# Attention products on TensorE tiles of 64 rows by 32 columns in place of 64 by 64

## The chip, the cores and the metric

The kernel runs on one core of a Trainium2 chip. The metric is the device time of one execution in microseconds. The kernel before takes 577.24 us, the median of three runs (577.07 to 577.51).

## What is computed

Attention with a sliding window and a linear position bias, followed by a gated MLP with spatial mixing. All inputs and outputs are float32. The shapes: 8 batches, 8 heads, 576 positions, 64 dimensions a head; the MLP has a model width of 512 and an inner width of 1024.

```python
def _attn_ref(q, k, v):
    B, H, S, D = q.shape
    window = 128
    scores = (1.0 / np.sqrt(D)) * np.matmul(q, k.transpose(0, 1, 3, 2))
    rel = np.arange(S)[:, None] - np.arange(S)[None, :]
    slopes = 2.0 ** (-8.0 * (np.arange(H) + 1) / H)
    bias = slopes[:, None, None] * (-np.abs(rel))[None, :, :]
    mask = (rel >= 0) & (rel < window)
    scores = np.where(mask, scores + bias[None], -1000000000.0)
    attn = softmax(scores)            # max, exp, sum, with 1e-9 added to the sum
    return np.matmul(attn, v)

def _moe_ref(x, w_in, g_ln, w_sg, b_sg, w_out):
    h = gelu_tanh(x @ w_in)
    u, v = h[..., :d_ff // 2], h[..., d_ff // 2:]
    v_n = (v - mean(v)) / np.sqrt(var(v) + 1e-06) * g_ln
    v_s = np.einsum('ts,bsd->btd', w_sg, v_n) + b_sg[None, :, None]
    return x + (u * v_s) @ w_out
```

A query at position s sees the keys s - 127 to s. So a block of 64 queries that begins at q0 needs the keys q0 - 127 to q0 + 63, at most 192 with the rounding to blocks, and a block of 32 needs at most 160.

## The kernel before, in words

The attention works on pairs of heads: 32 pairs n, four for each batch. The positions are cut into blocks of R = 64 (S = 576 is nine of them). For each pair there are single-letter steps: `q` and `L` load q, k and v; `a` and `c`, or `*` for both in one burst, make the scores; `A`, `B`, `C`, `G` (`minima`) add the bias and find each row's extreme; `e`, `E`, `f`, `F`, `j` take exponentials; `R` inverts the sums; `r`, `s`, `S` scale; `t`, `T`, `z` transpose on TensorE; `X`, `Y` mask; `V` (`values`) multiplies with v; `x`, `2`, `p` gather the result; `h`, `l`, `k` split it into a high and a low part for the MLP. The MLP of each batch follows in steps of its own (lines 609 to 611, 907, 942, 943, 1061), three products for each product of float32 accuracy.

The order of all steps is written out by hand in one long string, `ORDER`. On each engine instructions run in that order; the only freedom is when an engine waits for another. From pair 5 on, the scores of a pair are one step `*` (n >= 5), before that two steps `a` and `c`. For 16 of the later pairs the step `V` of pair n is written straight behind `*` of pair n + 2, and there the product of the first block of 64 positions goes into spare columns of that pair's last score bank.

Scores (`score_list`, lines 264 to 291). For t2 = 0 and t2 = 2 two PSUM banks of 512 columns are taken. A product has 64 queries of one head as its stationary operand (64 rows by 64 columns of the array) and up to 192 keys as its moving one. Head j lies on the rows j * 64 to j * 64 + 63, and its output goes to partitions 0 to 63 or 64 to 127, by `half ^ j`, so four tiles of the array are used. For each t2 there are eight products (two blocks i, two halves, two heads), and for t2 = 0 two more of 64 columns for the first 64 queries, which for `*` come before those of t2 = 2. In all 18 products a pair; each is float32 and shows as two matmul records and two weight loads. `burst` keeps the written order within a step.

Minima (`minima`, lines 297 to 307, on VectorE). In a bank the window of block i begins at column i * 192; the parts of the window that the mask cuts (the oldest and the own block) share 64 columns: `copy_predicated` puts the visible elements of the own block over the oldest one, so that 128 columns are left, on which two reductions run (a third for the first 64 queries).

Values (`values`, lines 368 to 392). The stationary operand is v (64 positions by 64 dimensions of one head), the moving one the masked, transposed weights of up to three blocks of queries, so up to 192 columns. Odd blocks k use the array's rows 0 to 63 and bank `x1[0]`, even ones rows 64 to 127 and bank `x1[1]`; the head gives the column half: again four tiles. Nine blocks by two heads are 18 products, and `first` adds two of 64 columns.

```python
for half in range(2):
    for j in range(2):
        q0 = (2 * t2 + 1 + i + 2 * half) * R
...
            insts.append(score(half, j, i * W, q0, q0 - P, q0 + R))
...
burst([part(k, c) for k in (0, 1, 2 * T, *range(2, 2 * T)) for c in cols] + [first(c) for c in cols])
```

## Time and profile before

| | us |
|---|---|
| median of three runs | 577.24 |
| lowest, highest | 577.07, 577.51 |
| the profiled execution's own time | 576.7 |
| its span in the profile | 575.0 |
| mean granted clock of TensorE | 0.997 |

The profile records every instruction of one execution. Engines are PE (TensorE's matmuls), PEld (its weight loads, which overlap the matmuls), DVE (VectorE), ACT (ScalarE), POOL (GpSimd) and SP (SyncE). A matmul's record is longer than the time for which it holds its tile: the records of consecutive matmuls overlap, so starts are to be compared, not ends. A line such as L278 is the line of the kernel in which the instruction was made. "Released by" is worked out from semaphores.

### The profile page before, as it was taken

To read this page: it belongs to the slowest core of one execution; us is meant where nothing else is said; L and a number is where in the kernel's file an instruction comes from. 1 tells how busy PE (TensorE), PEld (TensorE's weight loads), DVE (VectorE), ACT (ScalarE), POOL (GpSimd) and SP (SyncE) were. 2 spreads that over 40 slices of the span, in tenths; PEclk is the share of its full clock that TensorE was granted. 3 is DMA by queue.
4 is the path that set the end of the run, shared out by engine and by line. 5 is a ranking of instruction groups with operands and counts; after the bars stand their busy time and mean duration, and the time that the engine had idled before them with its cause. 6 is when DMAs were issued, how large, how long until landed. Compare 5 with 4: busy or idle time off the path is not lost.

```text
span 575.0 us, 14661 instructions
## 1 busy us (share of the span) xinstructions
PE 560.0 (97%) x5495; PEld 510.0 (89%) x5495; DVE 474.0 (82%) x1324; ACT 378.3 (66%) x1063; POOL 307.2 (53%) x365
## 2 busy tenths in 40 slices
PE   5899999999999999999999999999999999999997
PEld 4677899998899789998999998998999999998997
DVE  8989998799989778999787987878897988575646
ACT  7998997466844867567777576646695666733422
POOL 3676646520436544575338753496348653576325
PEclk9899999999999999999999999999999999999999
DMA  8675213216404413554260554136431606012502
GB/s 301 194 231 200 79 57 104 68 68 224 166 38 149 133 38 99 163 186 120 65 218 1 166 180 175 42 103 183 124 112 65 216 1 198 2 39 93 172 1 82
DMA packets 43561, 69.78 MB, mean 121 GB/s; under 512 B 3554, under 2 KB 31202, under 8 KB 43492
## 3 DMA queue, kind: packets, MB, share of 16 engines
q1 hardware_dynamic: 43492, 68.86, 36.7%
q8 instruction: 43, 0.70, 0.5%
q14 instruction: 26, 0.21, 0.1%
HBM read 56.27 MB, written 12.58 MB: 120 GB/s over the span
## 4 chain that ended last, share of the span: by engine, by line
PE 89%; DVE 4%; ACT 4%; DMA 2%; issue 1%; POOL 0%; SPq 0%; DVEq 0%; ACTq 0%
PE ps_m L609 13%; PE ps_m L1061 13%; PE ps_m L611 12%; PE ps_m L610 12%; PE ps_m L907 12%; PE ps_a L347 5%; PE ps_a L278 4%; PE ps_s L278 4%; PE ps_m L384 3%; PE ps_s L384 3%; PE ps_m L942 2%; PE ps_m L943 2%; ACT e L311 1%; PE ps_m L798 1%; PE ps_m L800 1%; DMA wst<-w_in 1%
## 5 line engine op out<-in xcount | busy, mean ns | idle before, releaser
L334 POOL TENSOR_TENSOR e<-e,rr 128x256 f32<-128x256 f32 (+2 forms) x116 | 80.6, 717 | 96.4 <-DVE rr L323 84.0
L311 ACT ACTIVATE e<-e,stats 128x128 f32<-128x128 f32 (+1 forms) x288 | 110.7, 387 | 17.2 <-DVE stats L295 16.6
L224 POOL TENSOR_TENSOR region<-u,region 128x288 fp32r<-128x288 f32 (+1 forms) x78 | 77.7, 1016 | 44.5 <-ACT region L1008 16.2
L356 DVE TENSOR_TENSOR px<-ps_a,m_both 128x1024 f32<-128x1024 f32 x64 | 77.4, 1216 | 5.4 <-PE ps_a L347 4.7
L609 PE MATMUL ps_m<-ws,region 128*128 128x288 f32 x256 | 78.3, 306 | 0.0
L611 PE MATMUL ps_m<-ws,region 128*128 128x288 f32 x256 | 75.9, 296 | 0.0
L610 PE MATMUL ps_m<-ws,region 128*128 128x288 f32 x256 | 75.6, 295 | 0.0
L732 POOL TENSOR_TENSOR rs<-rs,mhalf 128x1 f32<-128x1 f32 (+1 forms) x40 | 30.2, 756 | 57.5 <-DVE rs L729 57.3
L218 POOL TENSOR_TENSOR xs<-xf,xs 128x288 fp32r<-128x288 f32 (+1 forms) x48 | 49.9, 1060 | 13.8 <-ACT xs L403 13.8
L311 ACT ACTIVATION_READ_ACCUMULATOR e<-e,stats 128x1 f32 x288 | 54.5, 189 | 0.0
L1008 ACT ACTIVATE region<-u 128x576 fp32r<-128x576 f32 x35 | 23.7, 684 | 43.1 <-PE ps_m L610 17.5
L609 PEld LDWEIGHTS ps_m<-ws,region 128*128 128x128 f32 x256 | 48.3, 189 | 1.6 <-issue 0.8
L610 PEld LDWEIGHTS ps_m<-ws,region 128*128 128x128 f32 x256 | 48.3, 189 | 0.1
L611 PEld LDWEIGHTS ps_m<-ws,region 128*128 128x128 f32 x256 | 48.1, 188 | 0.2 <-DVE region L744 0.2
L609 PE MATMUL ps_m<-wi,xs 128*128 128x512 f32 x112 | 46.7, 417 | 0.1
L1068 DVE TENSOR_TENSOR xf<-ps_m,xf 128x576 f32<-128x576 f32 x48 | 35.8, 750 | 10.4 <-PE ps_m L1061 9.7
L611 PE MATMUL ps_m<-wi,xs 128*128 128x512 f32 x112 | 44.3, 396 | 0.0
L610 PE MATMUL ps_m<-wi,xs 128*128 128x512 f32 x112 | 44.2, 395 | 0.0
L347 PE MATMUL ps_a<-ident,e 128*128 128x128 f32 x256 | 38.6, 277 | 1.0 <-DVE px L356 1.0
L948 DVE TENSOR_TENSOR u<-ps_m,u 128x576 f32<-128x576 f32 x32 | 24.0, 753 | 18.2 <-PE ps_m L943 11.6
L278 PE MATMUL ps_s<-qk 64*64 64x192 f32 (+2 forms) x576 | 32.2, 338 | 5.5 <-DMA qk<-qkT 4.6
L295 DVE CUSTOM_DVE_ANT_0 e<-ps_s,bias 128x128 f32<-128x128 f32 (+1 forms) x140 | 34.9, 287 | 2.5
(217 smaller groups left out, 1591.8 us busy)
## 6 DMA issues: line engine op xcount, KB each, us to landing
qk<-qkT SPq DMA_DIRECT2D x32, 576.0 KB, 4.9
sum<-store SPq DMA_DIRECT2D x36, 512.0 KB, 4.7
outT<-xf SPq DMA_DIRECT2D x31, 288.0 KB, 3.0
vt<-v_in SPq DMA_DIRECT2D x32, 256.0 KB, 4.2
wst<-w_in SPq DMA_DIRECT2D x8, 512.0 KB, 5.2
store<-sum SPq DMA_DIRECT2D x6, 512.0 KB, 2.8
vt<-v_in SPq DMA_DIRECT2D x64, 32.0 KB, 3.8
wst<-w_out SPq DMA_DIRECT2D x4, 512.0 KB, 3.6
```

Source lines behind the costliest of these rows:

```text
L218: (engine or nc.gpsimd).tensor_tensor(out[:, cs], a[:, cs], b[:, cs], op)
L224: nc.gpsimd.tensor_tensor(out[:, fs], a[:, fs], b[:, fs], ALU.subtract)
L278: return lambda: nc.tensor.matmul(banks[half][to, c:c + k1 - k0], qk[js, 0, q0:q0 + R], qk[js, 1, k0:k1], start=True, stop=True)
L311: nc.scalar.activation(x, x, AF.Exp, bias=self.nm[0:n, i:i + 1], scale=-1.0, accum_out=self.sm[0:n, i:i + 1])
L334: nc.gpsimd.tensor_tensor(x[:, z:z + step, :], y[:, z:z + step, :], self.rr[0:n, i + z:i + z + min(k, step)].rearrange("p (m o) -> p m o", ...
L347: burst([lambda t=t: nc.tensor.transpose(cv[:, t // 2, t % 2], self.pr[j][:, t, :].rearrange("p (h c) -> p h c", h=2), ident[:, j * R:j * ...
L356: nc.vector.tensor_tensor(xv, cv, mv, ALU.mult)
L609: nc.tensor.matmul(dst, ah, bh, start=(first and i == 0), stop=False)
L610: nc.tensor.matmul(dst, ah, bl, start=False, stop=False)
L611: nc.tensor.matmul(dst, al, bh, start=False, stop=(last and i == n - 1))
L907: nc.tensor.matmul(dst, left(n, g, c)[:, ms], right(n, h, c), start=first and c == 0 and k == 0, stop=c == 1 and k == 2, skip_group_check= ...
L1061: nc.tensor.matmul(dst, p, q, start=first and f == 0 and k == 0, stop=f == 1 and k == 2, skip_group_check=True)
```

## The change

Scores and values are cut to tiles of 64 rows by 32 columns. A score product takes 32 queries and up to 160 keys; there are twice as many. A window is now laid out in the bank with a step of 160 columns (`BAND`), the rows of the second 32 queries 32 columns further on, and the first 64 queries' scores begin at column 352 (`LEAD`). For t2 = 0 the blocks i are taken in the order 1, 0, and the products of the first 64 queries come at the very end of the burst. `minima` addresses the same amounts of data through a new helper `window`. In `values` v is cut to 32 dimensions a product; the blocks k come in the order 1 to 7, 0, 8, the last together with the product of the first block. The string `ORDER` is not touched.

```diff
     XW = 2 * S + R
+    BAND = 5 * R // 2
+    LEAD = 2 * BAND + R // 2
+
+    def window(bank, c0, c1):
+        x = bank[:, c0:c0 + R].rearrange("p (t c) -> p t c", t=1)
+        return bass.AP(tensor=x.tensor, offset=x.offset, ap=[x.ap[0], [c1 - c0, 2], x.ap[2]])
...
         def scores(self, *t2s):
-            burst([x for t2 in t2s for x in self.score_list(t2, ps_a if len(t2s) > 1 and t2 == 0 else ps_s)])
+            insts = [x for t2 in t2s for x in self.score_list(t2, ps_a if len(t2s) > 1 and t2 == 0 else ps_s)]
+            burst(insts + (self.last_scores if 0 in t2s else []))
...
-            W = 3 * R
...
-            def score(half, j, c, q0, k0, k1):
-                js, to = heads[j], heads[half ^ j]
-                return lambda: nc.tensor.matmul(banks[half][to, c:c + k1 - k0], qk[js, 0, q0:q0 + R], qk[js, 1, k0:k1], start=True, stop=True)
+            half_block = R // 2
+
+            def score(half, j, c, q, k0, k1):
+                js, to = heads[j], heads[half ^ j].start + q % R
+                return lambda: nc.tensor.matmul(banks[half][to:to + half_block, c:c + k1 - k0], qk[js, 0, q:q + half_block], qk[js, 1, k0:k1], start=True, stop=True)
...
-            for i in range(2):
+            for i in (1, 0) if t2 == 0 else (0, 1):
                 for half in range(2):
                     for j in range(2):
-                        q0 = (2 * t2 + 1 + i + 2 * half) * R
-                        if q0 < P:
-                            insts.append(score(half, j, i * W + R, q0, 0, P))
-                        else:
-                            insts.append(score(half, j, i * W, q0, q0 - P, q0 + R))
+                        for z in (0, half_block):
+                            q0 = (2 * t2 + 1 + i + 2 * half) * R
+                            lo = max(q0 + z - P, 0)
+                            insts.append(score(half, j, i * BAND + lo - q0 + P, q0 + z, lo, q0 + z + half_block))
             if t2 == 0:
-                insts += [score(0, j, 2 * W, 0, 0, R) for j in range(2)]
+                self.last_scores = [score(0, j, LEAD, z, 0, R) for j in range(2) for z in (0, half_block)]
...
-            sv = bank.rearrange("p (b c) -> p b c", c=R)
             alone = t2 + j == 0
-            nc.vector.copy_predicated(sv[:, 0:6:5, :], sel_first if alone else sel, sv[:, 2:4, :])
+            nc.vector.copy_predicated(window(bank, 0, BAND + P), sel_first if alone else sel, window(bank, P, BAND))
...
-                self.shift(pr[j][:, t2 + i, :].rearrange("p (b c) -> p b c", b=2), sv[:, 4 * i:4 * i + 2, :], bs, nm[:, j * T + t2 + i:j * T + t2 + i + 1])
+                c = i * (BAND + R)
+                self.shift(pr[j][:, t2 + i, :].rearrange("p (b c) -> p b c", b=2), bank[:, c:c + P].rearrange("p (b c) -> p b c", c=R), bs, nm[:, j * T + t2 + i:j * T + t2 + i + 1])
...
-                self.shift(self.e0[:, R:P], sv[:, 6, :], bias[:, 0, :], nm[:, 2 * T:2 * T + 1])
+                self.shift(self.e0[:, R:P], bank[:, LEAD:LEAD + R], bias[:, 0, :], nm[:, 2 * T:2 * T + 1])
...
-                rows, slot, cs = slice(i * R, (i + 1) * R), (k + 1) // 2, slice(c, c + WIDE)
+                rows, slot, cs = slice(i * R, (i + 1) * R), (k + 1) // 2, slice(c, c + wide)
...
-                return lambda: nc.tensor.matmul(x1[i][cs, lo * R:hi * R], vt[rows, slot, cs], px[...], start=k < 2, stop=k in (2 * T - 2, 2 * T - 1), skip_group_check=True)
+                return lambda: nc.tensor.matmul(x1[i][cs, lo * R:hi * R], vt[rows, slot, cs], px[...], start=k in order[:2], stop=k in order[-2:], skip_group_check=True)
...
-            WIDE = D
-            cols = [c for j in (1, 0) for c in range(j * D, (j + 1) * D, WIDE)]
-            burst([part(k, c) for k in (0, 1, 2 * T, *range(2, 2 * T)) for c in cols] + [first(c) for c in cols])
+            wide = D // 2
+            order = [*range(1, 2 * T), 0, 2 * T]
+            cols = [c for j in (1, 0) for c in range(j * D, (j + 1) * D, wide)]
+            burst([part(k, c) for k in order[:-1] for c in cols] + [x for c in cols for x in (first(c), part(2 * T, c))])
```

## Rows read from the trace of the kernel before

**Rows 1.** The page, engines: busy us (share of the span) x instructions.
```profile
PE 560.0 (97%) x5495; PEld 510.0 (89%) x5495; DVE 474.0 (82%) x1324; ACT 378.3 (66%) x1063; POOL 307.2 (53%) x365
```

**Rows 2.** The page, the chain that ended last, share of the span by engine.
```profile
PE 89%; DVE 4%; ACT 4%; DMA 2%; issue 1%; POOL 0%; SPq 0%; DVEq 0%; ACTq 0%
```

**Rows 3.** Busy time by stretch: length, PE, PEld, DVE, ACT, POOL, clock, DMA, GB/s.
```profile
60.00:100.00 40.00, 40.00 (x450) 36.15 (x449) 36.50 (x113) 34.59 (x103) 24.66 (x24) 1.00 0.27 82
100.00:150.00 50.00, 50.00 (x527) 44.39 (x526) 44.67 (x138) 30.79 (x93) 16.55 (x19) 1.00 0.39 131
...
200.00:250.00 50.00, 50.00 (x518) 46.40 (x517) 41.17 (x125) 32.45 (x98) 25.45 (x26) 1.00 0.32 98
```

**Rows 4.** All waits of TensorE after 60 us: us in total, times, longest.
```profile
PE ps_m L907 <- PE ps_m L907: 0.9, 1, 0.9
PE ps_a L278 <- DMA qk<-qkT: 0.2, 1, 0.2
```

**Rows 5.** Timeline of TensorE, 229.2 to 231.3 us: start, us, line, operation, count.
```profile
229.01 0.30 PE L942 MATMUL ps_m<-wsA,vA 128*128 128x288 f32 x1
229.14 0.29 PE L943 MATMUL ps_m<-wsB,vB 66*128 66x288 f32 x1
229.37 0.88 PE L278 MATMUL ps_a<-qk 64*64 64x128 f32 x20
230.08 0.82 PE L278 MATMUL ps_s<-qk 64*64 64x192 f32 x16
230.83 0.40 PE L609 MATMUL ps_m<-ws,region 128*128 128x288 f32 x1
231.07 0.29 PE L610 MATMUL ps_m<-ws,region 128*128 128x288 f32 x1
```

**Rows 6.** Groups by line and shape, TensorE: busy us, mean ns of one | idle.
```profile
L384 PE MATMUL ps_m<-px,vt 64*64 64x192 f32 x408 | 25.3, 323 | 0.0
...
L384 PE MATMUL ps_m<-px,vt 64*64 64x128 f32 x136 | 13.1, 271 | 0.0
...
L384 PE MATMUL ps_m<-px,vt 64*64 64x64 f32 x68 | 4.8, 217 | 0.0
```

**Rows 7.** The same groups, weight loads of 128 and of 64 columns.
```profile
L609 PEld LDWEIGHTS ps_m<-ws,region 128*128 128x128 f32 x256 | 48.3, 189 | 1.6 <-issue 0.8 <-DVE u L948 0.3
...
L384 PEld LDWEIGHTS ps_m<-px,vt 64*64 64x64 f32 x612 | 20.7, 133 | 1.6 <-issue 0.2
```

**Rows 8.** Score records in the first 0.03 us of a burst: length, PE (records), PEld (records).
```profile
217.64:217.67 0.03, 0.03 (x4) 0.03 (x4) 1.00 0.00 0
```

**Rows 9.** Score products (L278) by stretch, the same columns.
```profile
60.00:250.00 190.00, 18.61 (x432) 13.55 (x432) 1.00 0.33 107
250.00:482.00 232.00, 22.96 (x540) 16.90 (x540) 1.00 0.39 125
```

**Rows 10.** Value products (L384) by stretch, the same columns.
```profile
60.00:250.00 190.00, 16.80 (x396) 12.30 (x396) 1.00 0.33 107
250.00:482.00 232.00, 22.23 (x540) 18.48 (x540) 1.00 0.39 125
482.00:515.00 33.00, 3.05 (x72) 2.21 (x72) 1.00 0.14 45
```

**Rows 11.** Timeline of TensorE, 478.2 to 481.9 us, scores of pair 31 and values behind.
```profile
479.20 0.82 PE L278 MATMUL ps_s<-qk 64*64 64x192 f32 x16
479.85 1.48 PE L384 MATMUL ps_m<-px,vt 64*64 64x192 f32 x36
```

**Rows 12.** Timeline of VectorE, 228.9 to 231.3 us: the first copy after a score burst.
```profile
230.33 0.30 DVE L302 COPY_PREDICATED ps_a<-sel,ps_a 128x128 f32<-128x128 uint8 x1 [1.16 <-PE ps_a L278]
```

**Rows 13.** Line 302 (the copy): its engine's idle before it, us, times.
```profile
  PE ps_a L278: 4.0, 4
  PE ps_s L278: 1.7, 2
```

**Rows 14.** Timeline of TensorE, 72.2 to 73.0 us: four transposes, untiled.
```profile
72.30 0.66 PE L347 MATMUL ps_a<-ident,e 128*128 128x128 f32 x4
```

## The prediction

> **What bounds the kernel now.** I read the busy times first, then the chain that ended last, then the busy time by stretch, then the waits. TensorE is busy for 560.0 of 575.0 us, VectorE for 474.0 [rows 1]; the chain is TensorE for 89% [rows 2]. A busy share alone would not prove a bound, since pipelined matmuls overlap in the records. But from 60 us on there is no hole: TensorE fills the stretches of 40 or 50 us to the hundredth [rows 3], and the list of what TensorE waited for after 60 us holds 1.1 us in all [rows 4]. So a nanosecond taken off TensorE's own stream after 60 us is a nanosecond of the span, until something else comes late. Nearest to that is VectorE: 36.5 of 40 us and 44.7 of 50 us up to 150 us, 41.2 of 50 later [rows 3]. Its steps stand in the same written order and move up with the matmuls they wait for.

> The attention products are the part that changes. A score burst of one pair is 36 matmul records (18 products in two passes each), 20 of them for query blocks 0 to 3 and then 16; the matmul before it starts at 229.14 and plain spacing is back at 231.07 [rows 5]: 1.93 us for what would be two plain steps, L943 to L609 to L610, of 0.13 us (L942 to L943 is 0.13). The burst thus takes some 1.67 us out of the chain. How much of that is streaming? The passes of the values product give the rate: 323, 271 and 217 ns for 192, 128 and 64 columns [rows 6], so (323 - 217) / 128 = 0.83 ns a column and pass, 1.66 ns for both passes. On each of the four tiles of 64x64 a pair streams 768 columns of scores (half 0: 128 + 192 + 64 + 192 + 192; half 1: four times 192; the granted clock is 1.00 in these stretches [rows 3], its upper level): 1.27 us. The remaining 0.40 us is the change of tiling on both sides, the first weights, and the spread of the starts. The four tiles do run at the same time: 36 passes of mostly 0.16 us of streaming would take over 5 us one after another.

> **The change part by part.**

> *Scores.* A block of 32 queries can see 128 + 32 = 160 keys; a block of 64 is given 192. There are now eight tiles (two heads by four blocks of 32 output rows), each with these columns: half 0, first 32 rows: 160 + 96 + 160 + 160 + 64 = 640; half 0, second 32 rows: 160 + 128 + 160 + 160 + 64 = 672; half 1: four times 160 = 640. The longest tile falls from 768 to 672. If eight tiles run side by side as four do, that is 96 x 1.66 = 159 ns less a pair. Weights: 128 columns load in 189 ns, 64 in 133 [rows 7], 56 ns for 64 columns, so a load of 32 is 28 ns shorter; only a burst's first is in the open: -28 ns. Four more tiles must be started: four matmuls and four loads are under way within 0.03 us of a burst's start [rows 8], at most 7.5 ns a pair of load and matmul, so at most +30 ns. Net -0.157, call it -0.16 us a pair. After 60 us there are 432 + 540 records [rows 9], over 36 = 27 pairs: 27 x 0.16 = 4.3 us. The five pairs before 60 us lie where the chain is not TensorE's alone; I count them at nothing (bound: 5 x 0.16 = 0.8 us gained).

> *Values.* Here only the tile's width changes, not the columns. A high tile (rows 64 to 127) streams 128 + 3 x 192 + 64 = 768 columns before and after, a low one 3 x 192 + 128, and the first block's 64 more. Per burst: -28 ns for the first weights where it doesn't follow scores directly, up to +30 ns for four more tiles. Zero, with 0.04 us either way as bounds; 396 + 540 + 72 records after 60 us [rows 10], over 36 = 28 pairs: -1.1 to +1.1 us. The new order of k (1 to 7, then 0, then 8 with the first block) gives both halves of the array equal lengths at each step, as the old one did in sum; I give it nothing by itself. What it keeps is the passage from scores to values: the last 16 score records start at 479.20, values at 479.85, with no hole between [rows 11], since both run in one tiling. With 64x32 for both that stays; it would be lost if only one had changed.

> *VectorE.* The predicated copy reads and writes the same 128x128 elements at other offsets; the three reductions keep their shapes: nothing. But the last two score products (now four), which write the same bank as the first block's, move from before the second 16 records to the very end of the burst. The first copy now starts at 230.33 [rows 12], 0.96 us after the burst's start at 229.37, and about 0.3 us after the last of the 20 started (group end 229.37 + 0.88, less a pass of 0.22). Afterwards the burst's last start is some 1.14 us in (672 columns, 1.11, plus load and spread, less the last 64 columns) and the copy some 1.44: 0.48 us later. Behind it on VectorE's queue stand the other copies and reductions of the pair and whatever block work is written next; ScalarE's exponentials wait for them. VectorE stood idle at that point 4 times for ps_a and 2 for ps_s, 5.7 us in all [rows 13]. Bounds: 0 (VectorE has 9% to 18% of slack) and 6 x 0.48 = 2.9 us (every such wait reaches TensorE). TensorE almost never waits for VectorE [rows 4], so I take 0.3 us.

> *Records.* 18 more score products and 20 more value products a pair, two passes each: 38 x 2 x 32 = 2432 more matmuls on the 5495 [rows 1], as many weight loads. They cost what is above if they are fed in time.

> *Sum.* Of 4.3 us I let 85% through (bounds 60% and 100%: TensorE is nearly the whole chain after 60 us [rows 4], but the written order has links that are just in time), 3.65, less 0.3: 3.3 us. The profiled execution took 576.7 us with its span of 575.0, so 573.4; the median of the runs shown, 577.24, is 0.5 above it, so 573.9.

> [...] In the first 0.03 us of a burst four matmuls are under way [rows 8], so starts on different tiles come 10 ns apart or nearer. [...]

> **The rivals.**
> - *Feeding (slower).* With eight tiles a pair of load and matmul must be issued every 134 / 8 = 16.7 ns (a pass of 160 columns is 133 ns), where now it is one every 1.21 / 36 = 34 ns (36 starts from 229.37 to 230.08 + 0.82 - 0.32 [rows 5]). If the steady pace is p, scores last 72 p and values 80 p, against 1.37 and 1.38 us now (first load to end of streaming: 1.21 + 0.16, and about the same for values). Over 27 and 28 pairs the change breaks even where 4184 p = 75.5 us: p = 18 ns. At 20 ns it loses 8.2 us: 585; at today's 34 ns 67 us: 644. The same holds if weight loads stop being hidden: ten passes a tile, each exposed by over 9 ns, and the gain is gone. For it: the densest places, scores straight into values [rows 11], would hold 304 records in 2.6 us, twice what the trace has anywhere. Against it: the starts of [rows 8].
> - *Shared stream (the change doesn't do what it says).* Four column tiles read the same 64 rows with four different moving operands; the trace shows two. If four share what serves two, scores take 2 x 1.11 and values 2 x 1.27: 27 x 0.95 + 28 x 1.27 = 61 us slower, 638. Against it: two share nothing measurable. An untiled transpose of 128 columns takes (0.66 - 0.28) / 3 = 0.13 us from start to start, first weights included [rows 14], no quicker a column than the tiled passes.
> - *Given back.* The gain is there on TensorE, but the later copy and VectorE up to 150 us (89 to 91% busy) take it: 4.3 - 2.9 - 1.1 leaves 0.3: 577.
> - *More.* The values gain their 0.04 as well and everything passes: 4.3 + 1.1 + 0.5 of the first pairs' 0.8: 571.3.

> **How the numbers follow.** Forecast (571.9 to 575.9) 0.60; more 0.06; given back, 575.9 to 578.5, 0.14; feeding 0.15, of which a fifth under 580; shared stream 0.05. Range 571.2 to 580.0: 0.60 + 0.05 + 0.14 + 0.03, 0.82. A measurement tells 0.2%, 1.15 us, from no change. Faster by more: 0.60 + 0.06 + 0.01 = 0.67. Within: 0.12. Slower by more: 0.15 + 0.05 + 0.01 = 0.21.

> **What would show it.** Right: a score burst with 72 records in place of 36 that takes 1.77 us between plain matmuls in place of 1.93, passes of 160 columns of about 296 ns, weight loads of about 105 ns, value bursts with 80 records as long as before, and the first copy some 1.4 us after the burst's start with TensorE still without holes. Feeding shows as starts 18 ns apart or more all through a burst; a shared stream as rounds of eight passes twice 134 ns. Given back shows as new holes on TensorE with VectorE as releaser. Wrong in size: pass-through, or the 0.40 us beside the streaming, which I leave as it is.

## The result, and the profile after

The changed kernel takes 584.71 us (median of 4 runs, 583.26 to 586.07) against 577.36 us (577.07 to 577.51) for the kernel before: the ratio is 1.0128 [1.0104, 1.0152], slower. The profiled execution is one of 585.54 us with a span of 583.7. The runs of one kernel now lie 2.8 us apart, where those of before lie 0.4 us apart. In the code after, the scores' matmul is L286 (L278 before), the values' are L391 and L395 (L384, L388), the copy is L308 (L302), the MLP's are L617 to L619 (L609 to L611), the transposes L354 and L367 (L347, L360).

Rows of the profile's page of after: engines, the queue that brings TensorE's instructions, and the chain by engine.

```profile
PE 558.8 (96%) x7927; PEld 510.2 (87%) x7927; DVE 473.6 (81%) x1324; ACT 379.0 (65%) x1063; POOL 308.8 (53%) x365
...
q8 instruction: 62, 1.02, 0.7%
...
PE 83%; DVE 7%; DMA 3%; POOL 2%; ACT 2%; issue 2%; SPq 1%; DVEq 0%; POOLq 0%; ACTq 0%
```

The 2432 additional matmuls are there, as many as were counted, and TensorE is busy 1.2 us less than in [rows 1]. But its share of the chain falls from 89% in [rows 2] to 83%, and VectorE's, DMA's and "issue" grow. So the loss is in idle time, not in work. The waits of TensorE after 60 us (total, times, longest), of which [rows 4] had two:

```profile
PE ps_s L395 <- issue: 1.8, 1, 1.8
PE ps_a L286 <- DMA qk<-qkT: 1.2, 2, 1.0
PE ps_m L915 <- issue: 1.1, 1, 1.1
PE ps_m L618 <- issue: 0.5, 1, 0.5
PE ps_a L354 <- POOL e L341: 0.5, 1, 0.5
PE ps_m L1069 <- issue: 0.5, 1, 0.5
PE ps_a L367 <- DVE px L363: 0.5, 1, 0.5
PE ps_a L354 <- DVE stats L302: 0.4, 1, 0.4
PE ps_m L617 <- DVE u L956: 0.4, 1, 0.4
```

The L915 row is the L907 row of [rows 4] and not new. The others are of two kinds. "Issue" is idle time in which TensorE waits for nothing that the profile shows: there is no releaser. Such idle time within a stream is called a hole here. The rest names VectorE, GpSimd or a transfer: work that now comes late. The longest hole after 60 us, in the timeline of TensorE, in the last products of a value burst:

```profile
487.89 0.27 PE L391 MATMUL ps_m<-px,vt 64*32 64x64 f32 x2
489.95 0.24 PE L395 MATMUL ps_s<-p,vt 64*32 64x64 f32 x1 [1.79 <-issue]
```

What can stop an engine in the middle of a burst whose operands have long been there? I counted all of TensorE's records (weight loads, matmuls and the 199 of its sequencer) in order of their starts. In order of time, the holes that begin at 33.0 (2.45 us from start to start), 450.9 (0.75), 468.3 (0.98) and 488.0 (the one above, 2.01) lie at records 960, 13504, 14016 and 14528, all of them 192 above a multiple of 256 to within two records; a fifth, of 0.33 us, is at 258.2, record 7616. The queue row gives the rest: 62 packets with 1.02 MB are 16.4 KB each, and the 16053 records less the first 192 are 256 a packet (before: 43 packets for 11205 records, 256 as well). So instructions arrive in blocks of 256 records, called pages from here on, and TensorE stood still at page ends: ahead of 489.95 an instruction packet starts at 487.44, takes 1.08 us, and work goes on 1.43 us after its end; for 450.9 and 468.3 it is 1.39 and 1.37 us. Scores straight into values hold 304 records in 2.6 us; the quickest page took 9.05 us before and 2.25 us after.

How long a hole is follows from how early the packet of the next page starts. At the four it starts 0.1, 1.9, 1.8 and 0.5 us ahead of the page's end; lead and hole together are 2.6, 2.6, 2.8 and 2.5 us. Over after and the runs e3, e4 and e9 below, 25 page ends had a packet with a lead under 2.45 us, and at each the sum is 2.2 to 2.8 us; the kernel before and e1, e2, e5 and e8, none of which has such a hole, have no lead under 2.55 us. So a page that is used up quickly is only one way to a hole: the page that ends at 33.0 lasted 5.97 us, but its successor's packet started 5.8 us into it. Long leads left no such hole: the shortest in before is 8.7 us, and at after's other page ends, with leads of 3.1 us and more, TensorE's records start at most 0.24 us apart.

A score burst by itself did what was forecast. One of them, timeline of TensorE, to be laid beside [rows 5]:

```profile
232.48 0.29 PE L951 MATMUL ps_m<-wsB,vB 66*128 66x288 f32 x1
232.70 0.75 PE L286 MATMUL ps_a<-qk 64*32 64x160 f32 x29
...
233.76 0.30 PE L286 MATMUL ps_a<-qk 64*32 64x64 f32 x7
234.00 0.40 PE L617 MATMUL ps_m<-ws,region 128*128 128x288 f32 x1
234.23 0.29 PE L618 MATMUL ps_m<-ws,region 128*128 128x288 f32 x1
```

From the matmul before it to plain spacing it is 1.75 us (232.48 to 234.23) where it was 1.93; 72 passes start within 1.145 us, 16 ns apart. VectorE's first copy of this pair, in VectorE's timeline, and, from the view of line 308, the idle time ahead of all ps_a copies after 60 us (us, times), which in the same stretch of before was 3.4 in 3 (the 4.0 in 4 of [rows 13] are of the whole run):

```profile
234.16 0.30 DVE L308 COPY_PREDICATED ps_a<-sel,ps_a 128x128 f32<-128x128 uint8 x1 [1.65 <-PE ps_a L286]
```

```profile
  PE ps_a L286: 9.8, 12
```

The copy starts 1.46 us after the burst's first product (232.70), where it was 0.96: later by 0.50 us. So it is, or by up to 0.65, in 13 of the bursts after 60 us; in most of the others VectorE came to the copy over 1 us into the burst before too.

### The profile page after: what moved, and what is told of

Same layout as the page of the kernel before. It is cut to its first block, busy times and chain, and to the rows that moved or that the text cites. A ratio compares the mean times of both kernels' runs of the same rounds, so it can differ in the third digit from the quotient of the medians.

```text
span 583.7 us, 19512 instructions
## 1 busy us (share of the span) xinstructions
PE 558.8 (96%) x7927; PEld 510.2 (87%) x7927; DVE 473.6 (81%) x1324; ACT 379.0 (65%) x1063; POOL 308.8 (53%) x365
## 3 DMA queue, kind: packets, MB, share of 16 engines
q1 hardware_dynamic: 43492, 68.86, 36.5%
q8 instruction: 62, 1.02, 0.7%
## 4 chain that ended last, share of the span: by engine, by line
PE 83%; DVE 7%; DMA 3%; POOL 2%; ACT 2%; issue 2%; SPq 1%; DVEq 0%; POOLq 0%; ACTq 0%
PE ps_m L1069 12%; PE ps_m L915 12%; PE ps_m L617 11%; PE ps_m L619 11%; PE ps_m L618 11%; PE ps_a L354 5%; PE ps_m L391 4%; PE ps_s L391 3%; PE ps_a L286 3%; PE ps_s L286 2%; DMA wst<-w_in 2%; DVE e L302 2%; PE ps_m L950 1%; PE ps_m L951 1%; PE ps_m L806 1%
## 5 line engine op out<-in xcount | busy, mean ns | idle before, releaser
L230 POOL TENSOR_TENSOR region<-u,region 128x288 fp32r<-128x288 f32 (+1 forms) x78 | 78.0, 1019 | 44.9 <-ACT region L1016 16.4
L617 PE MATMUL ps_m<-ws,region 128*128 128x288 f32 x256 | 78.3, 306 | 0.4 <-DVE u L956 0.4
L619 PE MATMUL ps_m<-ws,region 128*128 128x288 f32 x256 | 76.0, 297 | 0.0
L617 PEld LDWEIGHTS ps_m<-ws,region 128*128 128x128 f32 x256 | 48.3, 189 | 1.4 <-DVE u L956 0.5
L617 PE MATMUL ps_m<-wi,xs 128*128 128x512 f32 x112 | 46.6, 417 | 2.3 <-ACT xf L373 2.2
L619 PEld LDWEIGHTS ps_m<-ws,region 128*128 128x128 f32 x256 | 48.1, 188 | 0.7 <-DVE region L752 0.6
L619 PE MATMUL ps_m<-wi,xs 128*128 128x512 f32 x112 | 44.3, 395 | 0.1
L354 PE MATMUL ps_a<-ident,e 128*128 128x128 f32 x256 | 38.9, 276 | 2.4 <-DVE px L363 1.1
L286 PE MATMUL ps_s<-qk 64*32 64x160 f32 (+3 forms) x1152 | 32.0, 305 | 5.2 <-DMA qk<-qkT 4.6
L302 DVE CUSTOM_DVE_ANT_0 e<-ps_s,bias 128x128 f32<-128x128 f32 (+1 forms) x140 | 34.9, 287 | 2.5
```

Source lines behind the costliest of these rows:

```text
L230: nc.gpsimd.tensor_tensor(out[:, fs], a[:, fs], b[:, fs], ALU.subtract)
L286: return lambda: nc.tensor.matmul(banks[half][to:to + half_block, c:c + k1 - k0], qk[js, 0, q:q + half_block], qk[js, 1, k0:k1], start=Tru ...
L354: burst([lambda t=t: nc.tensor.transpose(cv[:, t // 2, t % 2], self.pr[j][:, t, :].rearrange("p (h c) -> p h c", h=2), ident[:, j * R:j * ...
L617: nc.tensor.matmul(dst, ah, bh, start=(first and i == 0), stop=False)
L619: nc.tensor.matmul(dst, al, bh, start=False, stop=(last and i == n - 1))
```

## The experiments

In each kernel the same MLP matmuls and transposes run in the same order, so every one can be paired with its counterpart in the trace of before, and the offset between the two followed. The table splits the final offset (us): what stood at 60 us, what the bursts' own steps changed after 60 us (only steps under 0.2 us: scores alone, 13 places; scores with values behind them, 15 places; values alone, 13 places), and all else, which is waits and holes. Waits are more than the lists show, since a delay of under 0.2 us stands in no list.

| kernel | at 60 us | scores alone | scores into values | values alone | waits and holes | at the end |
|---|---|---|---|---|---|---|
| after | 1.88 | -1.69 | -0.55 | 0.72 | 8.56 | 8.92 |
| e1_scores_narrow | -0.41 | -1.67 | -0.18 | 0.04 | 3.92 | 1.70 |
| e2_values_narrow | 0.13 | 0.03 | 2.64 | 0.65 | 0.00 | 3.45 |
| e4_last_scores_early | 2.22 | -0.62 | -0.60 | 0.66 | 6.79 | 8.45 |
| e5_narrow_scores_last_early | 0.07 | -0.59 | 1.06 | -0.01 | 0.53 | 1.06 |
| e8_narrow_scores_lead_in_other_bank | -0.23 | -1.81 | -0.28 | -0.01 | 0.76 | -1.57 |
| e9_after_lead_in_other_bank | 0.80 | -1.83 | -0.61 | 0.65 | 4.98 | 3.99 |

Two theories could explain the loss: F, that TensorE runs out of instructions at page ends where records stand too densely; and D, that work behind VectorE's later copies arrives too late.

**One half of the change at a time.** Only the scores on tiles of 64x32, values as before (last lines of the diff from after; `...` stands for lines left out):

```
...
-            wide = D // 2
-            order = [*range(1, 2 * T), 0, 2 * T]
...
-            burst([part(k, c) for k in order[:-1] for c in cols] + [x for c in cols for x in (first(c), part(2 * T, c))])
+            WIDE = D
...
+            burst([part(k, c) for k in (0, 1, 2 * T, *range(2, 2 * T)) for c in cols] + [first(c) for c in cols])
```

> The changed kernel with its values put back on 64x64 tiles in the old order; only the scores are on 64x32. Theory F (TensorE's instructions are fetched in pages of 256 records, and a page used up in under some 4.4 us leaves TensorE without instructions): scores followed by values are 144 + 80 = 224 records in place of 304, so no hole of over 0.3 us at a page's end is left; 27 score bursts at -0.17 us give 4.6 us, the change of tiling between scores and values costs some 0.2 us at 16 places, 3.2 us: 576 us. Theory D (the loss comes from the first scores' last products standing at the end of the burst, so that VectorE's first copy starts 0.5 us later): it is still late here, 580 us or more.

Measured: 579.06 us (578.28 to 579.33), ratio 1.0035 [1.0023, 1.0047]. And only the values on 64x32, scores as before (last lines of the diff from before):

```
...
-            WIDE = D
...
-            burst([part(k, c) for k in (0, 1, 2 * T, *range(2, 2 * T)) for c in cols] + [first(c) for c in cols])
+            wide = D // 2
+            order = [*range(1, 2 * T), 0, 2 * T]
...
+            burst([part(k, c) for k in order[:-1] for c in cols] + [x for c in cols for x in (first(c), part(2 * T, c))])
```

> The kernel before with only its values on 64x32 tiles in the new order. Theory F: 72 + 160 = 232 records behind each other, no holes at page ends; 28 value bursts at +0.05 us, 1.4 us, and 16 changes of tiling, 3.2 us: 582 us. Theory D: the copies start as before, so at most the 1.4 us: 577 to 579 us.

Measured: 580.27 us (579.78 to 580.44), ratio 1.0058 [1.0043, 1.0073]. Neither number was met: e1 lies between its two forecasts and so does e2. But neither trace has a hole over 0.3 us at a page end after 60 us. With 224 and 232 records where after has 304, their quickest pages took 4.98 and 4.73 us, so by the page theory it takes both halves together, and that is what happened. As a limit F's 4.4 us is not shown: in after pages of 2.25, 2.94 and 3.00 us left gaps of 0.22, 0.05 and 0.23 us. What e2 costs is all in the table's tile columns: 2.64 us at 15 passages from 64x64 to 64x32, 0.18 us each, where the first value products no longer start beside the last scores (0.25 us behind the last of them where it was 0.15), and 0.65 us at 13 lone value bursts, 0.05 us each. Its waits of TensorE are those of [rows 4] to 0.1 us. In e1 the bursts give 1.8 us and something else takes 3.9. Its waits of TensorE after 60 us, and its idle time ahead of the ps_a copies:

```profile
PE ps_m L914 <- issue: 1.1, 1, 1.1
PE ps_m L616 <- DVE u L955: 0.6, 1, 0.6
PE ps_a L367 <- DVE px L363: 0.5, 1, 0.5
PE ps_a L354 <- POOL e L341: 0.4, 1, 0.4
PE ps_a L354 <- DVE stats L302: 0.3, 1, 0.3
PE ps_a L286 <- DMA qk<-qkT: 0.3, 1, 0.3
```

```profile
  PE ps_a L286: 9.7, 12
```

The "issue" row and the transfer's are those of [rows 4]; the others are VectorE's and GpSimd's, the same as in after. So D stands as a second loss beside F.

**Holes moved by a shift.** After, with 64 small products (128 records) ahead of everything:

```
+    pre = ps_a.tile([P, 512], F32, name="ps_a")
+    for _ in range(64):
+        nc.tensor.matmul(pre[0:32, 0:2], spare[:, 0:32], spare[:, 0:2], start=True, stop=True)
```

> The changed kernel with 64 small products of 32x2 elements (128 records of matmul and weight load) put ahead of everything, while TensorE waits for its first data; all later work is the same. Theory F: the page ends move by half a page against the work. The holes without a releaser still lie at record numbers 192 above a multiple of 256, but at other scores and values: about 256, 313, 330, 350, 368, 401 and 418 us, no longer at 450, 468 and 488. Their sum changes by some us either way; worked out from the page times of the changed kernel's trace it is 11 to 14 us where that kernel's own comes out as 10: 583 to 589 us. Theory D: nothing moves, the same places are late and the time stays at 584.7.

Measured: 586.06 us (584.7 to 586.71), ratio 1.0158 [1.014, 1.0177]. The value burst that held after's longest hole runs through in one piece at 489.8, and nothing is left at 451 or 468. Holes stand instead at 51.0 (1.14 us from start to start), 262.3 (1.44), 318.0 (0.49), 335.2 (0.82) and 373.9 (1.11), again 192 above multiples of 256. The last of them in the timeline:

```profile
373.82 0.27 PE L391 MATMUL ps_m<-px,vt 64*32 64x64 f32 x2
374.99 0.21 PE L395 MATMUL ps_s<-p,vt 64*32 64x64 f32 x1 [0.89 <-issue]
```

The last four are four of the seven places named; at 350, 401 and 418 no hole came. That the place goes by the count of records and not by the data is shown; which of the dense page ends starve, and by how much, was not forecast well: the holes come to 5.0 us, where those of after are 6.5, and not to 11 to 14 and 10. That e3 is no faster even so lies in two other gaps that grew: those from start to start that end at 67.1 (GpSimd named) and 92.3 us (a transfer named) are 1.97 and 1.63 us, in after 0.76 and 0.52. The time by itself does not separate F from D here.

**The page's price by itself.** The kernel before, with 256 products of zeros, two columns each, on eight tiles of 64x32, ahead of everything (work added; the lines that make `zero` are left out):

```
...
+    pre = [ps_a.tile([P, 512], F32, name="ps_a") for _ in range(2)]
+    for k in range(256):
+        r, z = k // 4 % 2 * R, k % 4 * 32
+        nc.tensor.matmul(pre[k // 4 % 2][z:z + 32, 0:2], zero[r:r + R, :], zero[r:r + R, 0:2], start=True, stop=True)
```

> The kernel before with 256 products of zeros on eight tiles of 64x32, two columns each, ahead of everything else: 1024 records of weight load and matmul in a row (adds work, nothing left out). It measures the disputed cost by itself: how fast TensorE's instruction records come in when nothing else holds it. Theory F (pages of 256 records, about 4.4 us from crossing a page end to the next page's use): starts come in groups of 256 records with a hole after each group, about 4.4 us from one group's start to the next, while within a group records start 6 to 14 ns apart; the block takes 13 to 18 us and one instruction refill of about 1 us stands ahead of each hole's end. Rival D (records are issued at a steady pace, and the holes in after were waits for data): no holes, an even pace, 1024 records in about 8 us or less.

Measured: 591.59 us in its one run, and this timeline of TensorE:

```profile
1.05 2.19 PE L1238 MATMUL ps_a<-zero 64*32 64x2 f32 x223 [1.05 <-DVE zero L91]
8.04 1.35 PE L1238 MATMUL ps_a<-zero 64*32 64x2 f32 x128 [4.80 <-issue]
15.06 1.34 PE L1238 MATMUL ps_a<-zero 64*32 64x2 f32 x128 [5.67 <-issue]
18.79 0.42 PE L1238 MATMUL ps_a<-zero 64*32 64x2 f32 x33 [2.38 <-issue]
```

128 matmuls with their 128 loads are 256 records, one page, issued within 1.35 us (records about 5 ns apart, closer than the 6 to 14 of F), and then nothing: the groups start 7.0, 7.0 and 3.7 us apart, not 4.4. The block lasts 18.2 us, just above F's 13 to 18 and far from the 8 us of an even pace. Instruction packets of about 1 us start in it at 5.61, 12.70 and 16.19, and each of the later groups begins 1.2 to 1.5 us after one of them has ended. The first two start 2.6 and 3.5 us after the page's last record, the third at that record: the holes from start to start, 5.0, 5.9 and 2.6 us, are again that delay and 2.4 to 2.6 us.

**The copy's lateness.** First in after: the four products of the first 64 queries, on which the copy waits, go back ahead of the third block pair's.

```
-            burst(insts + (self.last_scores if 0 in t2s else []))
+            burst(insts)
...
-                self.last_scores = [score(0, j, LEAD, z, 0, R) for j in range(2) for z in (0, half_block)]
+                insts += [score(0, j, LEAD, z, 0, R) for j in range(2) for z in (0, half_block)]
```

> The changed kernel with the first 64 queries' score products back ahead of those of t2 = 2. Theory F: record counts and page ends are unchanged, the holes at 33, 451, 468 and 488 us stay, 583 to 585 us. Theory D: the first copy starts some 0.5 us sooner and the 3 us or so that VectorE's lateness costs come back: 580 to 582 us.

Measured: 583.81 us (582.12 to 585.42), ratio 1.012 [1.0093, 1.0148]: F's number. D's has failed as a number, but not its mechanism. The profiled execution is the slowest of the four, 585.42 us. VectorE's idle time ahead of the ps_a copies falls to 3.2 us in 3, and the transposes, 2.5 us late in after, are 0.25 us late. The gain went elsewhere in this trace: lone score bursts now end on passes of 160 columns and give 0.07 us, no longer 0.17; the holes over 0.3 us at page ends come to 5.0 us from start to start after 60 us where they were 4.1; and behind the longest one the clock fell. Busy time by stretch, with the clock in the third number from the right:

```profile
487.00:488.00 1.00, 0.11 (x4) 0.12 (x6) 0.00 (x0) 0.00 (x0) 0.60 (x2) 1.00 0.00 0
488.00:489.00 1.00, 1.00 (x12) 0.91 (x10) 0.04 (x1) 0.59 (x1) 0.00 (x0) 0.71 0.00 0
489.00:490.00 1.00, 1.00 (x7) 1.00 (x6) 1.00 (x2) 0.00 (x0) 0.00 (x0) 0.50 0.43 119
490.00:491.00 1.00, 1.00 (x6) 1.00 (x6) 1.00 (x2) 0.00 (x0) 0.00 (x0) 0.50 0.61 177
```

Behind the standstill of 2.05 us the granted clock is 0.71 in the microsecond from 488, 0.50 in the two after it, 0.59 in the next and 1.00 again from 492 on. The 12 products of L915 there last 3.16 us, against 1.75 us for the 12 that start at 479.86: 1.4 us more. In the trace of after the clock stays at 1.00 behind its hole of 1.79 us.

To see the lateness without holes, the same edit in e1 (values on 64x64):

```
-            burst(insts + (self.last_scores if 0 in t2s else []))
+            burst(insts)
...
-                self.last_scores = [score(0, j, LEAD, z, 0, R) for j in range(2) for z in (0, half_block)]
+                insts += [score(0, j, LEAD, z, 0, R) for j in range(2) for z in (0, half_block)]
```

> The narrow scores of e1_scores_narrow with values on 64x64 tiles, and the four products of the first 64 queries back ahead of the third block pair's products, where before has them. Theory L: of the 2.3 us by which e1 is slower than before, its score bursts give back about 1.9 us and lateness takes about 4 us: VectorE's first conditional copy starts up to 0.5 us later in each pair, because the four products on which it waits stand last in the burst, and the transposes and MLP steps behind it wait (transposes +2.8 us in e1's trace against before). With the four products early again that lateness goes (transposes within 0.5 us of before), the lone bursts end on long products and give 0.07 us each and no longer 0.17 (+1.1 us): 576.8 to 577.8, and VectorE's idle time ahead of the copies out of ps_a falls from 9.8 to under 5 us. Rival R: the lateness comes from the tile shape or from other engines and stays; then e5 is e1 plus 1.1 us, about 580.2.

Measured: 577.49 us (577.2 to 578.95), ratio 1.0007 [0.9998, 1.0016], inside L's range, and the idle time ahead of the ps_a copies is 3.5 us in all. Waits and holes fall from 3.92 to 0.53 us in the table. But a burst that ends on long products gives most of its gain away, at both kinds of places: -0.59 us where e1 has -1.67, and 1.06 where it has -0.18.

So the products should stay last, and VectorE not wait for them. In e1 again, they are written to the bank that it reads two copies later:

```
-            burst(insts + (self.last_scores if 0 in t2s else []))
+            burst(insts + (self.last_scores if (0 if self.n < FIRST else 2) in t2s else []))
...
-            if t2 == 0:
+            if t2 == (0 if self.n < FIRST else 2):
+                self.lead = banks[0]
                 self.last_scores = [score(0, j, LEAD, z, 0, R) for j in range(2) for z in (0, half_block)]
...
-                self.shift(self.e0[:, R:P], bank[:, LEAD:LEAD + R], ...)
+                self.shift(self.e0[:, R:P], self.lead[:, LEAD:LEAD + R], ...)
```

> e1_scores_narrow with the four products of the first 64 queries kept last in the burst, but written to the bank of the third and fourth blocks, which VectorE reads two copies later; only the reduction of these queries reads that bank (pairs 5 and up). Theory L: nothing that VectorE needs first stands last any more, and the burst still ends on short products: score bursts as in e1 (lone ones 0.17 us shorter than before, those ahead of values 0.02), lateness gone: 574.7 to 576.3, faster than before by 0.1 to 0.4%, VectorE's idle time ahead of the ps_a copies under 5 us. Rival R (lateness not from the place of these products): 578.5 to 579.5 as in e1. No stall of TensorE over 0.5 us at a page end is expected by either, since 224 records stand where after has 304.

Measured: 575.68 us (574.99 to 577.3) against 577.32 us for the kernel before in the same set, ratio 0.9978 [0.9969, 0.9986]: faster than before by 0.2%, 1.6 us between the medians, as theory L had it. Its waits of TensorE after 60 us, and its idle time ahead of the ps_a copies:

```profile
PE ps_m L915 <- issue: 1.1, 1, 1.1
PE ps_a L286 <- DMA qk<-qkT: 0.3, 1, 0.3
```

```profile
  PE ps_a L286: 2.0, 2
  ACT u L922: 0.8, 1
```

That is the list of [rows 4] again, within 0.2 us. The last run puts the same edit into the whole change, scores and values on 64x32; its diff from after is the one above:

> The changed kernel whole (scores and values on 64x32 tiles) with the one repair of e8_narrow_scores_lead_in_other_bank: the four products of the first 64 queries stay last, but go to the bank that VectorE reads two copies later. It splits the 7.5 us by which after is slower than before. Theory (two independent losses: about 6 us of page stalls and 3 to 4 us of lateness, against 2.3 us that the bursts give): the lateness goes and the stalls stay, 579.5 to 582; transposes within 0.5 us of before, VectorE's idle time ahead of the ps_a copies under 5 us (10.0 in after), and holes of 0.3 to 2.5 us at records 192 modulo 256 that sum to 4 to 7 us. Rival S (the lateness is only a consequence of the stalls): the time stays within 1 us of after, 584 to 585.5. Rival V (the lateness is what causes the holes): holes go too, 574 to 576.

Measured: 582.75 us (580.57 to 588.37), ratio 1.0124 [1.0093, 1.0155]; the upper end of the forecast was 582. By the ratio it is no faster than after (1.0128 [1.0104, 1.0152]), so what the repair gave here is read from one trace, that of its quickest run, 580.57 us. The waits of TensorE after 60 us, and VectorE's idle time ahead of the ps_a copies:

```profile
PE ps_s L396 <- issue: 1.9, 1, 1.9
PE ps_m L916 <- issue: 1.1, 1, 1.1
PE ps_m L392 <- issue: 0.8, 2, 0.5
PE ps_m L618 <- issue: 0.6, 1, 0.6
PE ps_a L286 <- DMA qk<-qkT: 0.5, 1, 0.5
```

```profile
  PE ps_a L286: 2.0, 2
  ACT u L923: 0.8, 1
```

VectorE and GpSimd are gone from the list, the holes are not: over 0.3 us and from start to start they are 4.1 us after 60 us and 1.33 us at 33. So in this trace the two losses are separate, and the rivals S and V fall. Runs of this kernel scatter by 7.8 us, more than those of any other; a hole of 2.1 us in the trace may be longer in another run, and the clock may fall behind it as in e4, but no trace of another run shows it.

## Why the prediction was wrong

The forecast was 573.9 us with a range to 580.0; it came to 584.71, on the side of its rivals.

- **Scores, -0.16 us a pair: right alone, less than half of it ahead of values.** Lone bursts gave 0.17 us; passes of 160 columns take 298 to 304 ns and loads of 32 columns 106 (296 and 105 forecast). Where values follow, scores and values together gave 0.07 us, and e1 shows 0.02 for the scores there. The step took the full 0.40 us beside the streaming as unchanged for all 27 bursts. But what a burst gains lies partly at its border: behind a last pass of 192 columns the next matmul starts 0.253 us after it (before), behind 160 columns 0.226, behind 64 columns 0.146 (after). Ahead of values that border was already 0.153 us. Instead of 4.3 us the scores gave about 2.2 (table, 1.69 + 0.55).
- **Values, zero with 0.04 either way: low.** Lone bursts are 0.05 us longer, 0.7 us in all: just outside the bound for one burst, inside the 1.1 us for all.
- **VectorE, 0.3 us: the term that was mis-sized.** The delay itself was right (0.48 forecast, 0.50 measured). But the price was put near the lower bound since TensorE almost never waited for VectorE in [rows 4]. That list shows what waits now, not what has room to be late. Copies that wait after 60 us went from 3 to 12, 3.4 to 9.8 us; e1 and e8 differ by this placement alone, and by 0.57% in their ratios, 3.3 us; the upper bound of 2.9 us would have been the better value.
- **Records, "They cost what is above if they are fed in time": the step that failed.** The condition was named and then counted as met. The rival *Feeding* had the right place, the 304 records from scores into values [rows 11], but the wrong mechanism: it priced a steady pace, with break-even at 18 ns. The pace was 16 ns in the scores and 17 in lone values, under break-even, as the starts of [rows 8] had suggested. What ran short was the next page of instructions: 4.1 us of holes after 60 us and one of 2.45 us at 33, where the term stood at nothing. Before, a page lasted 9 us or more, so [rows 4] could show no such wait. The profile's queue row, 43 packets of 16.4 KB, was there to be read; some 256 records a packet against 304 in 2.6 us would have given the question.
- **Shared stream** falls: a score burst of 72 passes would have lasted twice as long; its 72 starts lie within 1.145 us.
- **Given back** described half of what happened: the late copies did take more than the gain.

In the sum for the profiled executions, 8.9 us: the bursts gave 1.5 us after 60 us; 1.9 us had been lost by 60 us, in a hole of 2.45 us at 33; of the 8.56 us left about 4 are holes at page ends, and 3.6 to 4.5 are lateness behind the copies: 4.5 is what the holes leave, 3.6 the difference to e9, which has 4.98 without that lateness.

## What to carry to other kernels

Splitting products onto smaller tiles multiplies the instruction records, here from 11205 to 16053, and TensorE's came in pages of 256: count how long the densest 256 in a row last, since here kernels whose quickest page after 60 us lasted 4.7 us or more had no holes there, and those with 2.3 us had. Then look when the packet of the next page starts: in after leads of 0.1 to 1.9 us left holes of 2.45 to 0.33 us, leads of 2.3 and 2.4 us gaps of 0.22 and 0.23. When the order inside a burst is changed, ask which product the next engine's first step waits for; a bank that is read later took the late products for nothing (e8, 575.68 us, where e1 took 579.06). End a burst on its shortest passes where an untiled matmul follows: it started 0.146 us behind 64 columns, 0.253 behind 192.

## What the runs showed of the hardware

```profile
447.80:449.00 1.20, 1.20 (x76) 1.17 (x80) 1.03 (x2) 0.27 (x1) 1.06 (x2) 1.00 0.00 0
449.00:450.30 1.30, 1.30 (x88) 1.30 (x74) 1.30 (x3) 0.52 (x2) 0.81 (x1) 1.00 0.06 13
485.50:487.40 1.90, 1.90 (x119) 1.90 (x110) 1.28 (x5) 0.00 (x0) 1.90 (x4) 1.00 1.04 371
487.40:488.60 1.20, 0.76 (x46) 0.60 (x27) 1.17 (x10) 0.73 (x3) 1.20 (x3) 1.00 0.19 50
```

  The packet for the hole of 2.01 us starts as other transfers end, 1.8 us after its page was begun; the one for the hole of 0.75 us meets none and starts after 0.8 us. The same place holds the longest hole after 60 us in e4 and e9 (packets after 1.9 us). That the transfers hold the packet up is argued from this, not tested.
- Not every quick page starved: in after the one that ended at 436.65 lasted 2.25 us and left a gap of 0.22. Its successor's packet had started 2.3 us ahead, at 434.31, before the page itself was begun. What sets the start of a packet is open.
- Passes of 192 columns of float32 took 325 ns on tiles of 64x32 (after, L391 into ps_m), 323 on 64x64 [rows 6]. In after a lone score burst's 72 starts on eight tiles come 16 ns apart, 1.145 us in all.
- Passing from 64x64 to 64x32 took 0.18 us a time (e2, scores into values, 2.64 us at 15 places), 0.05 of which a lone value burst took too (0.65 us at 13). The other way, from narrow scores to wide values, the two bursts together took 0.18 us less than before at all 15 places (e1).
